# Inverting the first two chunks directly on VectorE, with loads from two queues and new due times, in a fused recurrence and MLP kernel

## The chip, the cores and the metric

One core of a Trainium2 chip runs the whole program. The metric is the device time in microseconds (us) of one execution, as the median of several. PE is TensorE, PEld its weight loads, DVE is VectorE, ACT is ScalarE, POOL is GpSimd, SP is SyncE, whose queue issues most transfers. "Clock" is TensorE's granted clock as a share of full speed. All runs quoted as fast lie within 1.5% of the fastest of the same kernel. The profiled execution is one of these runs; its span is a few us shorter than its time.

## The reference

```python
def _attn_ref(r, k, v, w, a, b):            # each [4, 8, 768, 40]
    state = zeros(B, H, D, D)
    for t in range(S):
        y[:, :, t] = einsum('bhd,bhde->bhe', rt, state)
        Sa = einsum('bhde,bhe->bhd', state, at)
        state = state * wt[..., None] - einsum('bhd,bhe->bhde', Sa, bt)
        state = state + einsum('bhd,bhe->bhde', vt, kt)
    return y

def _moe_ref(x, w_in, w_out):               # x: y as [3072, 320]
    h = x @ w_in                            # [3072, 2048]
    g = softplus(h)
    return g @ w_out
```

The kernel cuts the 768 time steps into 12 chunks of 64. Inside a chunk the recurrence becomes a triangular system, so a chunk needs the inverse of a unit triangular matrix per head and batch. Chunks hang together by the state alone. The MLP of a chunk (48 first-layer and 32 second-layer matmuls) can start when the chunk's y is there.

A word on correctness: the outputs are dominated by the MLP's weights, and y enters them weakly. The comparison therefore sees little of y.

## The kernel before

All operations are put into a graph. A list scheduler with a table of costs and a due time for each stage fixes the order on every engine when the program is built. On the chip each engine then works off its own queue in that order, waiting on semaphores:

```python
def emit(nc, stack, order):
    ...
    for o in order:
        for k, n in clock.waits(o):
            eng[o.eng].wait_ge(sem[k], n)
        ins = o.fn(o.eng)
        ...
```

Two chunks are inverted together by elimination in 60 dependent steps on GpSimd (the second engine choice, VectorE, is never taken, since chunks 0 and 1 go another way):

```python
NEUMANN = 2
NEAR = 4                       # buffers of kh, nh, gexc, aT, tlo
...
def invert(wd):
    e_, E_, cost = ("dve", V, ...) if wd == DVE_FW else ("pool", P, ...)
    op(dve(1900), [...], [mn], lambda e: V.transpose(m, mct), name="mt")
    for j in range(1, 31):
        nt = 31 - j
        op(cost(nt * j), [mn], ["mtmp"], lambda e: E_.tensor_tensor(tv, m[:, 0:j, j:j+1]..., ALU.mult))
        op(cost(nt * j), [mn, "mtmp"], [mn], lambda e: E_.tensor_tensor(m[...], m[...], tv, ALU.add))
    ...                        # mb: masked bf16 copy on the same engine
    op(dve(1100), [mbn], [dcn], ..., name="dc")     # transposed back on VectorE
    ...                        # dex: spread out, on ScalarE or VectorE
```

For chunks 0 and 1 the inverse is instead a product of powers on PE (`powers(c)`: squarings, and six apply steps in the chain). After that the chain of a chunk is W (the off-diagonal part), X, D, U, the state S and its transposes; then y, its transposes, and the MLP. All loads are issued from SyncE's queue, in a fixed list for the first four chunks; the two MLP weights come from GpSimd's queue. The MLP's h uses one PSUM bank, so ScalarE's exponential alternates with it.

Of the kernel before, what the change touches and what calls it, by code (L numbers as in the profile page):

```python
# [18 lines left out]
NEUMANN = 2  # L19
GT = 9  # L20
DVE_FW = 0
NQ = DFF // 128
# [41 lines left out]
class Graph:  # L64
# [43 lines left out]
    def deadlines(self):  # L108

        for (due, length), ops in self.stages.values():  # L110
# [7 lines left out]
PEN = 8.0  # L118
# [5 lines left out]
FILL, SAVE, MARGIN = 15000.0, 50000.0, 16  # L124
COUNT = {"tr": 8, "tot": 16, "gram": 32, "square": 32, "cum": 8, "W": 32, "X1": 16, "X": 32, "D": 32, "U": 32,
         "S1": 4, "S": 64, "sT": 32, "y1": 16, "y": 64, "yT": 6, "h": 6, "o": 4, "csb": 16, "apply": 36}
# [69 lines left out]
def schedule(ops):  # L196
# [16 lines left out]
    while ready:  # L213
# [84 lines left out]
        if o.dma:  # L298
            dmafree = max(dmafree, o.start + 900.0) + o.dma[1] * 25.4 / 16
            o.seen = dmafree + 1600.0  # L300
        else:
            o.seen = o.end + LAT[e]
# [30 lines left out]
def bass_rwkv7_goose__then__act_softplus_kernel(  # L333
# [17 lines left out]
    with ExitStack() as st:  # L351
# [51 lines left out]
        ginv = Ring("ginv", 2, [128, 2, DM], F32)  # L403
# [21 lines left out]
        mt = Ring("mt", 1, [128, 32, 32], F32)  # L425
        mtmp = sb("mtmp", [128, 240], F32)
# [17 lines left out]
        slt = sb("slt", [128, L], BF)  # L444
# [11 lines left out]
        def stage(name, i, start, length, c=None):  # L456
            g.tag = (name, i)
            g.stage = (PERIOD * ((i if c is None else c) + start), PERIOD * length)
# [10 lines left out]
        def pe(c):  # L469
            return {"pe": c}  # L470
# [21 lines left out]
        stage("const", 0, -4, 1)  # L492
# [30 lines left out]
        aff(fz[0][:, 0:128], fzn[0], 128, ALU.is_ge, 1.0, [[1, 128]], cm=-1)  # L523
        for x in X2:
            c = slice(64 * x, 64 * x + 64)
            op(dve(64), [fzn[0]], ["slt"], lambda e, c=c: V.tensor_copy(slt[c, :], fz[0][c, c]))
# [38 lines left out]

        def load(n, c):
            t, nm = RAW[n](c)
            side = F if n == "a" else G
            for bp in X2:
                for x in X2:  # L570
                    q = side(bp, x)
                    op({"sp": 800.0}, [], [nm + "%d%d" % (bp, x)],
                       lambda e, bp=bp, x=x, q=q: S.dma_start(  # L573
                           heads(t[q:q + 64, bp, :], D_),
                           SRC[n][2 * bp + x][:, c * L:(c + 1) * L, :].rearrange("h p d -> p h d")),
                       dma=(nm + "%d%d" % (bp, x), 512))

        def load_w(wd):
            t, nm = w_f(wd)
            for bp in X2:  # L580
                for x in X2:
                    q = G(bp, x)
                    op({"sp": 800.0}, [], [nm + "%d%d" % (bp, x)],
                       lambda e, bp=bp, x=x, q=q: S.dma_start(
                           heads(t[q:q + 64, bp, :], 2 * D_),
                           w[2 * bp + x][:, wd * 128:(wd + 1) * 128, :].rearrange("h (p z) d -> p h (z d)", z=2)),
                       dma=(nm + "%d%d" % (bp, x), 600))
# [5 lines left out]
        def load_weights():  # L593
            after = [kh(0)[1]]
            for q in range(3):
# [3 lines left out]
                   dma=("win%d" % q, 1500))  # L599
# [3 lines left out]
               dma=("wout", 4000))  # L603

        def setup_csb():
            stage("csb", 0, 1, 1)
# [118 lines left out]
        def logs(wd):  # L725
            stage("first", 2 * wd, -3, 1)
# [4 lines left out]
        def first(c):  # L731
            stage("first", c, -3, 1)
# [26 lines left out]
            if c < NEUMANN:  # L759
                return  # L760
# [17 lines left out]
        def power(kind, i):  # L778

            t, n = gT(i if kind == "M" else 6 + i % 2)  # L780
            return t[:, :, :].rearrange("p q m -> p (q m)").rearrange("p (b h m) -> p b h m", b=2, h=H_), n

        def powers(c):
            stage("powers", c, -0.5, 0.5)
            aT_, aTn = aT(c)
            nT_, nTn = nT(c)
            m, mn = power("M", 0)
            n, nn = power("N", 0)
            masked(grams(nT_, nTn, G, aT_, aTn, F), m, mn)
            masked(grams(aT_, aTn, F, nT_, nTn, G, F), n, nn, slt, "slt")  # L790
            for i in range(5):
                m, mn = power("M", i)
                n, nn = power("N", i)
                src, dst = (G, F) if i % 2 == 0 else (F, G)
                for kind, lhs, rhs in (("M", n, m), ("N", m, n)):
                    if kind == "N" and i == 4:
                        continue
                    t = Tile("a")

                    def f(bp, x, y, t=t, lhs=lhs, rhs=rhs, src=src, dst=dst):  # L800
                        q, o = src(bp, x), dst(bp, x)
                        return T.matmul(pf(t)[o:o + 64, bp, L * y:L * y + L], lhs[q:q + 64, bp, y, :],  # L802
                                        rhs[q:q + 64, bp, y, :])
                    op(pe(32 * 8.5), [mn, nn], [t], quads(f), mode=QUAD, name="square")
                    d, dn = power(kind, i + 1)
                    evac(1024, [t], [dn], lambda d=d: d, lambda t=t: bh(pf(t), L))


        def invert(wd):
            stage("invert", wd, -2.0, 1, 2 * wd)  # L810
            mct, mcn = mc(wd)
            m, mn = mt(wd)
            mbt, mbn = mb(wd)
# [5 lines left out]
            for j in range(1, 31):  # L819
                nt = 31 - j  # L820
                tv = mtmp[:, 0:nt * j].rearrange("p (a b) -> p a b", a=j)
                op(cost(nt * j), [mn], ["mtmp"],
# [3 lines left out]
                op(cost(nt * j), [mn, "mtmp"], [mn],  # L826
# [18 lines left out]
        def second(c):  # L845
            if c < NEUMANN:
                powers(c)
            stage("second", c, 0, 1)
# [56 lines left out]
            if c >= NEUMANN:  # L905
                t = Tile("a")

                def fw(bp, x, y, t=t):
                    q, o = F(bp, x), G(bp, x)
                    return T.matmul(pf(t)[o:o + 64, bp, L * y:L * y + 32], tl[q:q + 64, 32 * unit(bp, y):32 * unit(bp, y) + 64],  # L910
                                    de[q:q + 64, 16 * (c % 2) + unit(bp, y), 32:64])
                op(pe(32 * 8.5), [tln] + dens, [t], quads(fw), mode=QUAD, name="W")
                op(dve(512 * 1.04), [t, "wmask", "blk"], [wen],
                   lambda e, t=t: V.scalar_tensor_tensor(
                       we[:, :, :, 32:64].rearrange("p b h t -> p (b h) t"),
                       pf(t).rearrange("p b (h t) -> p (b h) t", t=64)[:, :, 0:32], blk[:, 0:1],
                       wmask[:, :].unsqueeze(1).to_broadcast([128, 16, 32]), ALU.mult, ALU.add))

            t = Tile("a")

# [32 lines left out]
            if c >= NEUMANN:  # L953
                t = Tile("a")

                def fy0(bp, x, y, t=t):
                    q, o = F(bp, x), G(bp, x)
                    return T.matmul(pf(t)[o:o + 64, bp, col(y)], de[q:q + 64, 16 * (c % 2) + unit(bp, y), :],
                                    x_[q:q + 64, bp, col(y)])
                op(pe(32 * 8.5), pair(xn) + dens, [t], quads(fy0), mode=QUAD, name="D")  # L960
                chain_evac(t, y_, yn, "De")
                t = Tile("a")

                def fu(bp, x, y, t=t):
                    q = G(bp, x)
                    return T.matmul(pf(t)[q:q + 64, bp, col(y)], we[q:q + 64, bp, y, :], y_[q:q + 64, bp, col(y)])  # L966
                op(pe(32 * 16.0), pair(yn) + [wen], [t], quads(fu), mode=QUAD, name="U")
                chain_evac(t, u_, un, "Ue")
            else:
                cur, cn, cs = x_, xn, F  # L970
                for step, (i, dst) in enumerate(((1, G), (0, F), (3, G), (2, G), (4, F), (5, G))):
                    m, mn = power("M", i)
                    nxt, nn_ = (u_, un) if step == 5 else ((y_, yn), (x_, xn))[step % 2]
                    t = Tile("a")

                    def fa(e, t=t, m=m, cur=cur, cs=cs, dst=dst):
                        for bp, x in ALL:
                            q, o = cs(bp, x), dst(bp, x)
                            T.matmul(pf(t)[o:o + 64, bp, 0:DM], eye(q), cur[q:q + 64, bp, 0:DM],
                                     start=True, stop=False)  # L980
                        for y in range(H_):
                            for bp, x in ALL:
                                q, o = cs(bp, x), dst(bp, x)
                                j = T.matmul(pf(t)[o:o + 64, bp, col(y)], m[q:q + 64, bp, y, :],
                                             cur[q:q + 64, bp, col(y)], start=False, stop=(y == H_ - 1))
                        return j
                    op(pe(290.0 + 32 * 8.5), pair(cn) + [mn, "ident"], [t], fa, mode=QUAD, name="apply")
                    chain_evac(t, nxt, nn_, "Ae")
                    cur, cn, cs = nxt, nn_, dst

# [48 lines left out]

            t = Tile("a")  # L1040
# [35 lines left out]
        def mlp(c):  # L1076
            stage("mlp", c, 1, 1)
            xT_, xTn = xT(c)
            gts = [gT(8 + c * 4 + x) for x in range(4)]
# [52 lines left out]
        for wd in range(NCH // 2):  # L1132
# [6 lines left out]
            if wd == 0:  # L1139
                pass  # L1140
            if 2 * wd >= NEUMANN:
                invert(wd)
# [44 lines left out]
```

## Time and profile before

| | before |
|---|---|
| median (3 runs given) | 393.62 us (391.86 to 393.98) |
| span of the profiled run, mean clock | 388.8 us, 0.854 |
| GpSimd's first elimination step | 93.1 us |
| first MLP matmul | 61.2 us |
| second MLP | 123.7 us |

The first part of the page gives each engine's busy time, its share of the span and its number of instructions:

```profile
PE 308.8 (79%) x8512; PEld 231.6 (60%) x8512; DVE 218.8 (56%) x360; ACT 217.0 (56%) x312; POOL 202.4 (52%) x358
```

No engine is full over the run.

### The profile page before, as it was taken

How to read it: one execution, taken by the hardware profiler on the slowest of the kernel's cores; microseconds unless marked ns; L12 is line 12 of the kernel's file. 1: busy time of each engine (PE TensorE's matmuls, PEld its weight loads, DVE VectorE, ACT ScalarE, POOL GpSimd, SP SyncE). 2: the span in 40 equal slices, each digit the busy share in tenths (PEclk: the TensorE clock that was granted, in tenths of full speed). 3: DMA queues.
4: the chain of work that ended last, by engine and by line, in shares of the span. 5: the costliest groups of instructions: out<-in, count | busy, mean ns of one | idle time of the engine just before them, and what ended most of it. 6: DMA issues, size and time to landing. Idle time of an engine off the chain costs nothing.

```text
span 388.8 us, 18635 instructions
## 1 busy us (share of the span) xinstructions
PE 308.8 (79%) x8512; PEld 231.6 (60%) x8512; DVE 218.8 (56%) x360; ACT 217.0 (56%) x312; POOL 202.4 (52%) x358
## 2 busy tenths in 40 slices
PE   0565868885688777999888869999789995999864
PEld 0454655554566445777666657777567774676542
DVE  7864642277746336676748667766663655554101
ACT  2435434557425751678865665584665747365651
POOL 6120101003989859978699954999757885000000
PEclk9855565996855988699999987999969997899997
DMA  6797996766765721476646553503202200101001
GB/s 122 123 186 139 131 150 117 141 104 111 138 104 104 120 55 27 65 120 111 120 80 110 89 96 63 88 5 71 37 19 54 55 21 3 35 4 38 18 18 34
DMA packets 145742, 31.35 MB, mean 81 GB/s; under 512 B 140224, under 2 KB 145344, under 8 KB 145664
## 3 DMA queue, kind: packets, MB, share of 16 engines
q1 hardware_dynamic: 143232, 27.55, 40.6%
q0 software_dynamic: 2432, 2.62, 4.2%
q8 instruction: 66, 1.08, 1.1%
q14 instruction: 12, 0.10, 0.1%
HBM read 28.84 MB, written 3.93 MB: 84 GB/s over the span
## 4 chain that ended last, share of the span: by engine, by line
PE 50%; DVE 15%; POOL 13%; issue 9%; ACT 8%; SPq 2%; DMA 1%; POOLq 1%; DVEq 0%; ACTq 0%
PE ps L1106 12%; PE ps L1087 11%; PE ps L636 7%; POOL mt L827 5%; POOL mtmp L823 4%; ACT gT L1096 4%; ACT et L1093 3%; POOL mb L831 2%; PE ps L698 2%; PE ps L657 2%; PE ps L802 2%; SPq L573 2%; PE ps L1056 2%; PE ps L1031 1%; PE ps L966 1%
## 5 line engine op out<-in xcount | busy, mean ns | idle before, releaser
L823 POOL TENSOR_TENSOR mtmp<-mt 128x30 f32<-128x30 f32 (+9 forms) x150 | 78.4, 523 | 57.6 <-DVE mt L818 47.1
L1093 ACT ACTIVATE et<-ps 128x512 f32<-128x512 f32 x96 | 57.1, 595 | 63.4 <-PE ps L1087 63.1
L1087 PE MATMUL ps<-xT,win 128*128 128x256 bf16 x576 | 84.6, 286 | 7.3 <-ACT et L1093 6.3
L827 POOL TENSOR_TENSOR mt<-mt,mtmp 128x30 f32<-128x30 f32 (+9 forms) x150 | 84.6, 564 | 11.0
L1106 PE MATMUL ps<-wout,gT 128*128 128x320 bf16 x384 | 68.0, 315 | 8.6 <-ACT gT L1096 7.3
L1087 PEld LDWEIGHTS ps<-xT,win 128*128 128x128 bf16 x576 | 53.5, 102 | 22.3 <-ACT et L1093 10.6
L1096 ACT ACTIVATE gT<-et,hln 128x1024 bf16<-128x1024 f32 x48 | 55.2, 1149 | 1.2
L1106 PEld LDWEIGHTS ps<-wout,gT 128*128 128x128 bf16 x384 | 34.7, 101 | 26.5 <-ACT gT L1096 10.8
L1111 DVE TENSOR_TENSOR osb<-ps,csb 128x320 f32<-128x320 f32 x24 | 11.8, 490 | 32.1 <-PE ps L1106 32.1
L889 POOL CAST v_b<-v_f 128x640 bf16<-128x640 f32 x12 | 8.6, 721 | 20.2 <-DMA v_f<-in_v_dram 18.3
L473 ACT ACTIVATE gT<-ps 128x1024 bf16<-128x1024 f32 x11 | 11.3, 1024 | 11.8 <-PE ps L802 11.7
L473 ACT ACTIVATE xb<-ps 128x320 bf16<-128x320 f32 x20 | 8.3, 435 | 17.0 <-PE ps L931 9.6
L1062 DVE TENSOR_TENSOR yo<-ps,gexc 128x640 bf16<-128x640 f32 x12 | 9.9, 825 | 12.1 <-PE ps L1056 12.0
L669 DVE TENSOR_TENSOR pt<-ps,sut 128x1024 bf16<-128x1024 f32 x12 | 14.6, 1218 | 3.7 <-PE ps L657 3.7
L669 DVE TENSOR_TENSOR qt<-ps,sut 128x1024 bf16<-128x1024 f32 x12 | 14.6, 1220 | 3.1 <-PE ps L657 3.1
L802 PE MATMUL ps<-gT 64*64 64x64 bf16 x576 | 10.2, 226 | 7.8 <-issue 4.2
L473 DVE COPY rT<-ps 128x1024 bf16<-128x1024 bf16 x10 | 6.9, 692 | 16.5 <-PE ps L636 16.5
L698 PE MATMUL ps<-lw,nexc 64*64 64x320 bf16 x96 | 8.3, 402 | 9.1 <-DVE ninc L508 9.1
L1022 DVE TENSOR_TENSOR state<-ps,gtot 128x320 bf16<-128x320 f32 x22 | 9.8, 486 | 9.1 <-PE ps L1014 9.0
L669 DVE TENSOR_TENSOR tak<-ps,sut 128x1024 bf16<-128x1024 f32 x12 | 14.6, 1215 | 0.4 <-PE ps L657 0.4
L750 DVE SCALAR_TENSOR_TENSOR nh<-b_f,ginv 128x640 bf16<-128x640 f32 x12 | 12.0, 998 | 4.7 <-ACT ginv L746 4.7
L831 POOL TENSOR_TENSOR mb<-mt,fmask 128x1024 bf16<-128x1024 f32 x5 | 13.9, 2786 | 0.4
(145 smaller groups left out, 604.3 us busy)
## 6 DMA issues: line engine op xcount, KB each, us to landing
w_f<-in_w_dram SPq DMA_DIRECT2D x24, 160.0 KB, 3.4
a_f<-in_a_dram SPq DMA_DIRECT2D x48, 80.0 KB, 3.1
b_f<-in_b_dram SPq DMA_DIRECT2D x48, 80.0 KB, 3.2
k_f<-in_k_dram SPq DMA_DIRECT2D x48, 80.0 KB, 3.1
v_f<-in_v_dram SPq DMA_DIRECT2D x48, 80.0 KB, 3.2
r_f<-in_r_dram SPq DMA_DIRECT2D x48, 80.0 KB, 3.1
out_dram<-osb SPq DMA_DIRECT2D x48, 80.0 KB, 2.1
wout<-in_moe_w_out_dram POOLq DMA_DIRECT2D x1, 1280.0 KB, 13.5
```

What stands on the lines that cost most here:

```text
L473: return A.activation(o, i, AF.Copy) if e == "act" else V.tensor_copy(o, i)
L636: i = T.transpose(pb(t)[:, bp, off + 128 * yy:off + 128 * yy + 128], src[:, bp, 128 * yy:128 * yy + 128], ident[:, :])
L669: lambda e: V.tensor_tensor(parity(dst), bh(pf(t), L), bc4(mask[:, :], L), ALU.mult), name="mask")
L698: i = T.matmul(pf(t)[s:s + 64, bp, 0:DM], mats[z][q:q + 64, :], heads(lwt[q:q + 64, bp, :], 2 * D_)[:, :, z * D_:z * D_ + D_], start=(z == ...
L802: return T.matmul(pf(t)[o:o + 64, bp, L * y:L * y + L], lhs[q:q + 64, bp, y, :], rhs[q:q + 64, bp, y, :])
L823: lambda e, j=j, nt=nt, tv=tv: E_.tensor_tensor(tv, m[:, 0:j, j:j + 1].to_broadcast([128, j, nt]), m[:, j:j + 1, j + 1:32].to_broadcast([1 ...
L827: lambda e, j=j, tv=tv: E_.tensor_tensor(m[:, 0:j, j + 1:32], m[:, 0:j, j + 1:32], tv, ALU.add))
L831: lambda e: E_.tensor_tensor(mbt[:], m[:, :, :].rearrange("p s (t e) -> p t s e", e=2), fmask[:, :, :].rearrange("p s (t e) -> p t s e", e ...
L1087: i = T.matmul(one(t)[:, 256 * (q % 2):256 * (q % 2) + 256], win[:, z, q * 128:(q + 1) * 128], xT_[:, z, :], start=(z == 0), stop=(z == 2))
L1093: lambda e, q2=q2, t=t, ett=ett: A.activation(ett[:, q2 % 2, :], one(t), AF.Exp), name="exp")
L1096: lambda e, q2=q2, ett=ett: A.activation(gts[q2 // 2][0][:, :, :].rearrange("p q m -> p (q m)"), ett[:, :, :].rearrange("p q m -> p (q m)" ...
L1106: i = T.matmul(one(t)[:, 0:DM], gts[z][0][:, q % 4, bp * 128:(bp + 1) * 128], wout[:, q, :], start=(q == 0), stop=(q == NQ - 1))
```

## The change

Its intent: the squarings of chunks 0 and 1 block the start, and GpSimd idles for 93 us. Now VectorE eliminates chunks 0 and 1 while GpSimd, as soon as it can, does 2 and 3; the squaring goes. The first loads come from two queues in the order in which the inverses need them. Every stage gets its own due time.

```diff
-NEUMANN = 2
-GT = 9
+GT = 8
 DVE_FW = 0
+FIRST = ["w0", "w2", "b0", "a0", "b1", "b2", "a1", "b3", "a2", "k0", ...]
+BY_ACT = ("a2", "b0", "b1", "v0", "v3",)
+DUE = {"const": (-5.361, 3.246), "csb": (1.398, 0.376), "logs": (-1.996, 1.066), ...}
+EARLY = {("invert", 0): -7.569, ("first", 0): -6.798, ...}
...
-        mt = Ring("mt", 1, [128, 32, 32], F32)
-        mtmp = sb("mtmp", [128, 240], F32)
+        mt = Ring("mt", 2, [128, 32, 32], F32)
+        mtmp = Ring("mtmp", 2, [128, 240], F32)
...
+        def issuers(n, c):
+            return {"act" if "%s%d" % (n, c) in BY_ACT else "sp": 680.0}
...
-        def powers(c):            # and the apply steps of the chain: all removed
...
-            if 2 * wd >= NEUMANN:
-                invert(wd)
+            invert(wd)
```

Cut: the scheduler's constants (PEN 8.0 to 10.48, the modelled sizes of transfers), the names of the stages, and a third buffer for ginv.

## The prediction

> **What bounds the kernel now.** I read, in order, the page (busy shares and the 40 slices), the longest waits, the timeline of the first 110 us, the ten-microsecond windows, and then single groups of matmuls. The slices of the page (one slice is 9.72 us; digits are busy tenths):
>
> ```profile
> PE   0565868885688777999888869999789995999864
> DVE  7864642277746336676748667766663655554101
> POOL 6120101003989859978699954999757885000000
> PEclk9855565996855988699999987999969997899997
> ```
>
> TensorE (PE) is busy 103 of the first 150 us (sum of the windows), much of that at half clock; from the 17th slice on it is nearly full. GpSimd (POOL) does nothing until slice 9, then works almost without a pause until slice 33. It runs five inversions, each for two chunks (64 steps of time each); by the timeline they lie at 93.1-133.4, 139.4-180.9, 186.9-226.9, 237.7-277.7 and 284.7-323.5 us. The waits:
>
> ```profile
> POOL mtmp L823 <- DVE mt L818: 47.1, 5, 29.7
> ...
> DVE dc L834 <- POOL mb L831: 14.7, 5, 3.9
> ```
>
> GpSimd waited 29.7 us for its first matrix, and its results were late five times. Each such lateness is a hole in PE (windows: start:end, length, PE, PEld, DVE, ACT, POOL busy, clock, DMA share, GB/s):
>
> ```profile
> 240.00:250.00 10.00, 9.60 (x346) 7.56 (x348) 6.71 (x11) 3.38 (x5) 9.01 (x17) 1.00 0.41 77
> 250.00:260.00 10.00, 9.69 (x303) 7.66 (x296) 7.17 (x12) 8.06 (x13) 8.98 (x14) 1.00 0.17 29
> ...
> 280.00:290.00 10.00, 7.05 (x152) 4.83 (x150) 6.88 (x9) 6.22 (x9) 5.11 (x14) 0.66 0.07 18
> ...
> 320.00:330.00 10.00, 5.81 (x159) 4.51 (x157) 4.83 (x7) 6.75 (x10) 5.99 (x11) 0.83 0.01 2
> ```
>
> **The start and the loads**, from the timeline (start, length):
>
> ```profile
> 0.81 2.78 SPq L584 DMA_DIRECT2D w_f<-in_w_dram  x4
> ...
> 17.17 0.82 DVE L752 TENSOR_TENSOR kh<-k_f,ginv 128x640 bf16<-128x640 f32 x1
> 18.29 1.80 POOL L598 DMA_DIRECT2D win<-in_moe_w_in_dram  x3 [11.10 <-DVE kh L752]
> ...
> 19.91 9.19 SPq L573 DMA_DIRECT2D b_f<-in_b_dram  x4
> ...
> 61.17 1.46 PE L1087 MATMUL ps<-xT,win 128*128 128x256 bf16 x6 [0.65 <-DVE xT L473]
> ```
>
> The first MLP matmul, which is the only large filler PE has, comes at 61.2 us. One queue needs about 2.7 us for four issues; chunk 1's b is fully issued only at 29.1, because the weights' transfers squeeze in. The squared-matrix route of chunks 0 and 1 then fills 20-110 us with dependent small matmuls and copies: state 1 comes at 110, the second MLP at 123.8, and chunks 2 and 3 wait for the inversion that ends at 133. By 160 us 100 of 576 first-layer matmuls are done (2.1 chunks of MLP).
>
> **PE's work at full clock.** From start-to-start times of whole groups between 160 and 340 us: six first-layer matmuls 0.655, four second-layer ones 0.545; a chunk has 8 of each, 9.6 us. The rest of a chunk: six 8-matmul transposes at 0.46 (2.8), four gram groups at 0.28 (1.1), cumulative sums and totals 1.1, W 0.55, X 0.55, D 0.28, U 0.62, state 0.93, its transposes 0.55, y 0.83, yT 0.34: also 9.6. Check: in 240-280 us there are 90 first-layer, 60 second-layer matmuls and two chunks of the rest, 1.88 x 9.6 + 2 x 9.6 = 37 of 40 us, a ratio of 1.07. In 160-340 us there are 360, 228 and eight chunks: 147 of 180 us, a ratio of 1.22. The difference is GpSimd's lateness and the clock after it.
>
> **What the Trainium skill says.** "TensorE: Matmul & The Clock Gate", Part 1: the clock is halved by default and released after some 3.4 us of activity; the trace agrees (0.50 in 20-50 us, 1.00 in 240-280). "VectorE: DVE Perf Modes", the errata section: an fp32 tensor_tensor takes (N+151)/0.96 ns; N = 640 gives 824, the trace has 815-818 with GpSimd idle. "GPSIMD Engine Reference", Specifications: its SBUF interfaces are shared with VectorE, with contention where VectorE has two SBUF inputs. The trace agrees: kh takes 0.82 us while GpSimd idles and up to 1.27 beside an inversion, and GpSimd's 240-element step, usually 0.62, took 1.08 when hit. "Trainium Kernel Development and Optimization", Key Constraints: all issuing queues share 16 DMA engines; more queues save issue time only. The trace has 122 GB/s at a DMA share of 0.66-0.77 from one queue and 177 at 0.98, so the second queue can gain at most about 1.4 times.
>
> **The change, part by part.**
> *Removed:* 576 squaring matmuls (10.2 us of PE), the apply steps (5.9 + 8.5), two gram groups (about 1); on ScalarE and VectorE their copies (11.3 and 8.6 us), four masks (4.9) and 24 half-tile copies (about 11). *Added:* W, D, U for two chunks (3.9 us of PE), and on VectorE one inversion. PE's busy time falls by about 22 us, but mostly by work in time that was half idle; what counts is the new path.
> *VectorE's inversion:* 60 tensor_tensors on 9920 elements in all: (9920 + 60 x 151)/0.96 = 19.8 us, plus 60 ns per dependent step as between its dependent memsets, 3.6: 23.4 us alone. But the order of the changed kernel puts other VectorE work inside it. The first matrix: two queues deliver a and b of chunks 0 and 1 by about 12 us; ah and nh (0.82 each), transposes at half clock (1.03), copies, grams, mc and mt (1.9) follow: the inversion starts about 25. Its first 36 steps (6384 elements, 14.5 us) are mixed with thirteen other operations (11.2 us) and in-order waits for loads, csb and wout (5 us, a guess): 56. Then mt of chunks 2 and 3 (1.9) starts GpSimd at about 58, not 93. The last 24 steps (8.8 us) and two kh (1.6) then meet GpSimd's steps: with 0.4 us each, as kh lost, another 10 us: 78. Mask, transpose and dex add 3.5, D and U to y, xT another 9: **first MLP at about 90 us, 29 us later than before.** That is the price.
> *What is gained:* at that point PE has already prepared chunks 0-3, both chains 0 and 1 are nearly through, and the next inversion is 35 us ahead. By the order of PE's instructions, left then are 12 MLPs (115), 10 chains (W, X, D, U, state and its transposes, 3.5 each: 35), 11 outputs (a transpose, a gram, y, yT, 1.9 each: 21), 10 preparations of k, v, r (three transposes, two grams, totals, 2.2 each: 22) and most of 8 of a, b (two transposes, a gram, sums, 2.05 each: 15): 208 us at full clock. GpSimd: 30-34 us of steps, 4.7 of gaps, 2.8 of mask, casts: about 41 per inversion, against about 2 x 19.2 x 1.1 = 42 of PE for two chunks. It keeps pace, tightly. I take 1.14, between 1.07 and 1.22: 237 us. The last MLP's alternation with ScalarE and the last stores add 8. Span 90 + 237 + 8 = 335. Before, the median time was 4.8 us above the profiled span (393.6 against 388.8): **340 us, 14% less.**
>
> **Rivals.** *The late first MLP decides:* if inversion, collisions and in-order waits take till 105 and the pace stays at 1.22, 105 + 254 + 13 = 372 (5% faster). For: VectorE does everything in order, and the wait for wout, which took 13.5 us to land, is inside it. Against: by 90 us the old kernel had little to show for its early start. *GpSimd stays the bound:* each of its four later inversions ends after PE wants it. From 58 us, 50 for the first with collisions and 4 x 46 give 292, then 50 us for the last two chunks (some 37 us of listed work after their D, by 1.15, and the 8 of the end): 342 span, 347 us. For: 41 against 42. Against: without the 29.7 us idle it has a head start. *Loads are hidden anyway:* the second queue brings nothing, as the shared engines are the limit; the inversion starts 5 us later: 345. *PE saturates cleanly* at 1.07 and the first MLP comes at 82: 82 + 223 + 13 = 318.
>
> **Range and chances.** First MLP 80-102 and ratio 1.07-1.22 span 316-369 at the corners; the middle 8 in 10 is 324 to 360. Being within 2% of before (over 386) needs both corners exceeded by 17 us; schedules fixed by a cost table can misfire, so 4% for same and slower together.
>
> **What would show it.** Right: GpSimd's first step at 50-65 us instead of 93; first MLP at 80-100; PE at 9 tenths or more from about 100 to the end, clock 1.00; the wait of GpSimd for mt under 25 us in total after its start; VectorE's inversion steps clearly longer after GpSimd starts. Wrong: PE holes of over 3 us before each D, at 45 us spacing (GpSimd binds); a first MLP after 105; or a long wait of VectorE for DMA within its inversion.

## The result, and the profile after

| | before | after |
|---|---|---|
| median of the same rounds (4 runs each) | 392.74 us (391.27 to 393.98) | 365.95 us (363.65 to 366.5) |
| span of the profiled run, mean clock | 388.8 us, 0.854 | 361.9 us, 0.890 |
| GpSimd's first elimination step | 93.1 us | 61.15 us |
| first MLP matmul | 61.2 us | 99.5 us |
| second MLP | 123.7 us | 121.5 us |

The ratio is 0.9318 (95% interval 0.9265 to 0.937). Ratios here are the mean time of one kernel's fast runs over that of the other's of the same rounds, so not quite the ratio of the medians quoted. The kernel is 6.8% faster; 14% was predicted, and 366 lies outside the range of 324 to 360.

The page after, busy times and the slices (one slice is 9.05 us):

```profile
PE 276.6 (76%) x7632; PEld 211.0 (58%) x7632; DVE 236.4 (65%) x415; ACT 203.1 (56%) x291; POOL 202.1 (56%) x356
...
PE   0544542048898999787999979899969999899873
...
DVE  7679729985679787676468696575954567475201
...
POOL 6010112896782078998899831899886888300000
PEclk9975855555589999999999999999996999999999
```

PE lost 32 us of busy time against the page before and the span 27. GpSimd now starts in the seventh slice. But it has two holes (slices 13 and 14, 24 and 25), which an engine that binds would not have, and PE's clock is at half from the sixth to the eleventh slice although PE is busy at eight tenths in the last two of these. From there up to the last slices PE has 6 to 9 tenths, not a steady 9.

The start, in the timeline (start, length, then what ended the idle time before it):

```profile
27.44 0.19 DVE L812 TENSOR_TENSOR mtmp<-mt 128x30 f32<-128x30 f32 x1
...
52.10 0.82 DVE L773 TENSOR_TENSOR kh<-k_f,ginv 128x640 bf16<-128x640 f32 x1 [7.10 <-DMA k_f<-in_k_dram]
...
61.15 0.29 POOL L812 TENSOR_TENSOR mtmp<-mt 128x30 f32<-128x30 f32 x1 [10.97 <-DVE mt L807]
...
73.83 2.34 PE L719 MATMUL ps<-lw,ninc 64*64 64x320 bf16 x16 [17.13 <-ACT lw L750]
...
74.17 0.66 DVE L812 TENSOR_TENSOR mtmp<-mt 128x30 f32<-128x30 f32 x1
...
79.02 0.62 PE L946 MATMUL ps<-xb,dex 64*64 64x40 bf16 x32 [2.85 <-DVE dex L831]
...
99.48 1.46 PE L1054 MATMUL ps<-xT,win 128*128 128x256 bf16 x6
```

VectorE's inversion starts at 27.4 and its result enters D at 79.0. In between it stands 7.1 us for k, and its last steps run beside GpSimd's: a step on 30 elements took 0.19 us at the start and 0.66 us at 74.2. PE waits 17 us for a logarithm of chunk 4, whose w landed late. From D to the first MLP it takes 20.5 us.

The windows (start:end, length, PE, PEld, DVE, ACT, POOL busy, clock, DMA share, GB/s):

```profile
80.00:90.00 10.00, 8.10 (x310) 7.11 (x308) 5.32 (x11) 3.37 (x6) 6.59 (x12) 0.50 0.90 165
90.00:100.00 10.00, 8.50 (x261) 6.51 (x254) 6.70 (x8) 4.48 (x8) 7.86 (x11) 0.50 0.56 104
...
240.00:250.00 10.00, 9.90 (x268) 7.47 (x267) 5.42 (x10) 6.30 (x10) 9.06 (x15) 1.00 0.33 62
250.00:260.00 10.00, 10.00 (x328) 8.17 (x329) 8.36 (x12) 7.26 (x12) 9.14 (x14) 1.00 0.26 45
260.00:270.00 10.00, 7.10 (x108) 4.66 (x96) 6.74 (x8) 5.21 (x8) 8.63 (x19) 1.00 0.15 34
280.00:290.00 10.00, 9.52 (x385) 7.22 (x383) 6.33 (x11) 4.27 (x8) 8.93 (x15) 1.00 0.53 94
```

In 80-100 us PE looks busy, at half clock. In 260-270 there is a hole like those of the kernel before: the D of chunk 8 (270.5) waits for GpSimd's fourth inversion, which ended at 265.1.

The waits (engine, operation, line, then what it waited for; us in total, times, longest):

```profile
ACT et L1060 <- PE ps L1054: 49.2, 53, 3.0
...
PE ps L719 <- ACT lw L750: 29.5, 2, 17.1
POOL v_b L876 <- PE ps L980: 26.5, 5, 10.5
...
POOL mtmp L812 <- DVE mt L807: 19.6, 3, 11.0
...
DVE dc L823 <- POOL mb L820: 5.0, 3, 3.0
```

GpSimd waited 19.6 us for its matrices, 47.1 before, of which 11.0 are the start. It also waited 26.5 us before casts of v, which stand in its queue behind PE's state product. By the timeline GpSimd's inversions lie at 61.1-106.8, 127.6-166.9, 170.0-208.4, 225.8-265.1 and 268.1-307.5. So the gaps are 20.8, 3.1, 17.4 and 3.0 us; each holds the masked copy mb, which takes 2.8 us on GpSimd.

**Where PE's time went.** I multiplied every matmul of the trace with the unit cost of the prediction (W at its full-clock 0.27 us, see below). From 100 to 340 us that gives 191 of 240 us. The other 49 us are: 19.3 at 178 places where PE goes from full-array to quarter-array tiles or back without any idle time (0.11 us each), 25.4 at 34 places where it idles, and 4.4 spread thin.

### The profile page after: what moved, and what is told of

The parts are those of the page before. It is cut to its first block, busy times and chain, and to the rows that moved or that the text cites. A ratio compares the mean times of both kernels' runs of the same rounds, so it can differ in the third digit from the quotient of the medians.

```text
span 361.9 us, 16900 instructions
## 1 busy us (share of the span) xinstructions
PE 276.6 (76%) x7632; PEld 211.0 (58%) x7632; DVE 236.4 (65%) x415; ACT 203.1 (56%) x291; POOL 202.1 (56%) x356
## 4 chain that ended last, share of the span: by engine, by line
PE 34%; POOL 23%; DVE 16%; ACT 8%; issue 7%; SPq 5%; ACTq 3%; DMA 2%; POOLq 1%; DVEq 0%
POOL mt L816 10%; POOL mtmp L812 10%; PE ps L1054 9%; PE ps L1073 9%; PE ps L657 5%; SPq L594 4%; ACT gT L1063 3%; DVE mtmp L812 3%; ACTq L594 2%; DVE mt L816 2%; DVE mt L807 2%; PE ps L954 2%; PE ps L678 2%; PE ps L980 2%; ACT et L1060 2%
## 5 line engine op out<-in xcount | busy, mean ns | idle before, releaser
L812 POOL TENSOR_TENSOR mtmp<-mt 128x30 f32<-128x30 f32 (+9 forms) x150 | 79.2, 528 | 30.2 <-DVE mt L807 19.6
L816 POOL TENSOR_TENSOR mt<-mt,mtmp 128x30 f32<-128x30 f32 (+9 forms) x150 | 83.0, 553 | 11.1
L1054 PE MATMUL ps<-xT,win 128*128 128x256 bf16 x576 | 81.1, 278 | 5.5 <-ACT et L1060 4.5
L1073 PE MATMUL ps<-wout,gT 128*128 128x320 bf16 x384 | 63.7, 300 | 6.7 <-ACT gT L1063 4.2
L1054 PEld LDWEIGHTS ps<-xT,win 128*128 128x128 bf16 x576 | 51.9, 99 | 17.6 <-ACT et L1060 8.4
L876 POOL CAST v_b<-v_f 128x640 bf16<-128x640 f32 x12 | 8.6, 717 | 37.2 <-PE ps L980 26.5
L719 PE MATMUL ps<-lw,ninc 64*64 64x320 bf16 x96 | 11.3, 371 | 17.1 <-ACT lw L750 17.1
L750 ACT ACTIVATE lw<-w_f 128x1280 bf16<-128x1280 f32 x6 | 7.6, 1273 | 22.5 <-DMA w_f<-in_w_dram 13.5
L719 PEld LDWEIGHTS ps<-lw,ninc 64*64 64x64 bf16 x96 | 5.8, 132 | 19.8 <-ACT lw L750 17.3
L773 DVE TENSOR_TENSOR kh<-k_f,ginv 128x640 bf16<-128x640 f32 x12 | 12.1, 1008 | 7.1 <-DMA k_f<-in_k_dram 7.1
L771 DVE SCALAR_TENSOR_TENSOR nh<-b_f,ginv 128x640 bf16<-128x640 f32 x12 | 14.3, 1190 | 2.2 <-ACT ginv L767 2.2
L876 POOL CAST r_b<-r_f 128x640 bf16<-128x640 f32 x12 | 9.3, 775 | 10.6 <-DMA r_f<-in_r_dram 9.8
```

Source lines behind the costliest of these rows:

```text
L719: i = T.matmul(pf(t)[s:s + 64, bp, 0:DM], mats[z][q:q + 64, :], heads(lwt[q:q + 64, bp, :], 2 * D_)[:, :, z * D_:z * D_ + D_], start=(z == ...
L771: lambda e: V.scalar_tensor_tensor(hd(n_), bh(bf_, D_), -1.0, bh(gi, D_), ALU.mult, ALU.mult))
L812: lambda e, j=j, nt=nt, tv=tv: E_.tensor_tensor(tv, m[:, 0:j, j:j + 1].to_broadcast([128, j, nt]), m[:, j:j + 1, j + 1:32].to_broadcast([1 ...
L816: lambda e, j=j, tv=tv: E_.tensor_tensor(m[:, 0:j, j + 1:32], m[:, 0:j, j + 1:32], tv, ALU.add))
L876: lambda e, dst=dst, src=src: P.tensor_copy(hd(dst), bh(src, D_)), name="cast")
L1054: i = T.matmul(one(t)[:, 256 * (q % 2):256 * (q % 2) + 256], win[:, z, q * 128:(q + 1) * 128], xT_[:, z, :], start=(z == 0), stop=(z == 2))
```

## The experiments

Each kernel ran beside the kernel before, whose median was 389 to 395 us, most on different chips; so ratios are compared with the changed kernel's 0.9318, and differences under about 1% are not resolved. Unless the text says that the order is another, it is frozen on every engine as in the changed kernel: the scheduler keeps its old costs, and only what the chip does changes. All runs behind the ratios are fast ones; the medians are of all four runs, with one slow run in warm_through, two in local_four and one in local_five.

| run | median us | ratio to before | 95% interval |
|---|---|---|---|
| changed kernel | 365.95 | 0.9318 | 0.9265 to 0.937 |
| old_no_squaring | 380.8 | 0.975 | 0.9683 to 0.9818 |
| one_queue | 373.71 | 0.958 | 0.95 to 0.9661 |
| pool_light | 357.28 | 0.9169 | 0.9097 to 0.924 |
| mlp_light | 367.88 | 0.9431 | 0.9366 to 0.9496 |
| mlp_thin | 364.27 | 0.9287 | 0.9244 to 0.9331 |
| both_light | 351.08 | 0.8926 | 0.8853 to 0.8998 |
| mlp_heavy | 374.18 | 0.957 | 0.9504 to 0.9636 |
| dve_light | 363.94 | 0.9231 | 0.9161 to 0.9302 |
| fast_start | 370.7 | 0.9405 | 0.9321 to 0.9489 |
| warm | 367.49 | 0.9357 | 0.9317 to 0.9397 |
| warm_through | 374.32 | 0.9549 | 0.9459 to 0.9639 |
| cast_act | 363.73 | 0.9312 | 0.9246 to 0.9379 |
| cast_dve | 365.88 | 0.9369 | 0.9301 to 0.9436 |
| due_search | 373.97 | 0.9535 | 0.9507 to 0.9564 |
| local_four | 383.04 | 0.9712 | 0.963 to 0.9795 |
| local_five | 380.5 | 0.9716 | 0.9669 to 0.9764 |

### Which part of the change brings what

**old_no_squaring**: the kernel before with the inversion on VectorE alone (the scheduler ran anew on it, with the old due times).

```diff
-NEUMANN = 2
-GT = 9
+NEUMANN = 0
+GT = 8
-        mt = Ring("mt", 1, ...); mtmp = sb("mtmp", ...)
+        mt = Ring("mt", 2, ...); mtmp = Ring("mtmp", 2, ...)
```

> The kernel before with one part of the change alone: chunks 0 and 1 inverted on VectorE like the others on GpSimd, no squaring, the rings of the inversion's tiles as in the changed kernel; loads and due times stay as they were. If the inversion on VectorE is the part that brings the gain: 360 to 375 us. If the due times and load order carry it: 385 to 400 us, with GpSimd's first step still near 90 us.

**one_queue**: the changed kernel with all loads issued from SyncE.

```diff
         order = schedule(g.ops)
+        for o in order:
+            if o.dma and o.eng == "act":
+                o.eng = "sp"
```

> The changed kernel with every load issued from SyncE's queue, in the same order; nothing else changes. My prediction's rival (loads hidden anyway, the 16 shared engines are the limit): 366 to 371 us, the first MLP matmul at 99 to 104 us. If the second queue matters: the inversion on VectorE starts 5 or more later than 27.4 us and the time is 372 or more. If the loads on ScalarE's own queue cost more than they bring (ScalarE's first Ln waited till 11.1 us behind its twelve issues, 6.4 in the kernel before): under 364 us.

Measured: 380.8 and 373.7. GpSimd's first step in the timeline of old_no_squaring, then of one_queue:

```profile
74.97 0.83 POOL L824 TENSOR_TENSOR mtmp<-mt 128x30 f32<-128x30 f32 x1 [11.37 <-DVE mtmp L824]
```

```profile
67.82 0.28 POOL L812 TENSOR_TENSOR mtmp<-mt 128x30 f32<-128x30 f32 x1 [10.64 <-DVE mt L807]
```

So the step goes from 93.1 to 75.0 by leaving the squaring out, to 67.8 by the new order and due times (with a third buffer for ginv), and to 61.15 by the second queue; the ratio goes 1, 0.975, 0.958, 0.9318. All three parts count, with 2.5, 1.7 and 2.6 points (the first is clear of 1 by its interval, but not surely over 2%). My expectation for old_no_squaring missed both its ranges; that for one_queue got the time right, but VectorE's inversion started at 30.9, 3.5 us later and not 5. The rival "loads are hidden anyway" (5 us in the prediction) falls: the second queue is worth 2.6 points, some 10 us. The order of one_queue was made for two queues, though; an order of its own might lose less, and was not run. The price of the second queue is visible too. ScalarE issues twelve loads before its first logarithm, which starts at 11.09 us, 6.38 in the kernel before (timelines, before and after):

```profile
6.38 1.27 ACT L729 ACTIVATE lw<-w_f 128x1280 bf16<-128x1280 f32 x1 [4.30 <-DMA w_f<-in_w_dram]
...
11.09 1.27 ACT L750 ACTIVATE lw<-w_f 128x1280 bf16<-128x1280 f32 x1 [9.00 <-issue]
```

### What sets the pace: GpSimd, PE or neither

**pool_light** (wrong result): GpSimd's steps on one row.

```diff
-                       tv, m[:, 0:j, j:j + 1]...
+                u = 1 if wd != DVE_FW else j
+                       tv[:, 0:u, :], m[:, 0:u, j:j + 1]...     # the addition likewise
```

> The changed kernel, but each elimination step on GpSimd works on one row instead of j rows (same instructions, order and waits; the result is wrong on purpose). GpSimd's inversions then take about 20 instead of 39.5 us. Theory GpSimd (its inversions, with the ring of four buffers behind them, set the pace of PE): 15 us or more faster than the changed kernel, 350 us or less. Theory PE (PE's own work, mode switches and in-order queue set the pace, GpSimd only fits in): within 6 us, 360 to 366 us. It also takes away GpSimd's collisions with VectorE, worth some us in either theory.

**mlp_light** (wrong): two contraction parts instead of three.

```diff
-                        for z in range(3):
+                        for z in range(2):
```

> The changed kernel with two instead of three contraction parts in each first-layer matmul group: 192 of 576 such matmuls less, 0.11 us each, 21 us of PE work removed, same order (the result is wrong on purpose). Theory PE: 16 to 21 us faster than the changed kernel, 345 to 350 us. Theory GpSimd: PE's gaps before each D only grow, 0 to 8 us faster, 358 to 366 us.

**mlp_thin** (wrong): the third part on 32 columns, with every instruction kept.

```diff
+                            n = 256 if z < 2 else 32
-                            i = T.matmul(one(t)[:, 256 * (q % 2):256 * (q % 2) + 256], ..., xT_[:, z, :], ...)
+                            i = T.matmul(one(t)[:, 256 * (q % 2):256 * (q % 2) + n], ..., xT_[:, z, 0:n], ...)
```

> As the light MLP, but with the number of instructions kept: the third contraction part of each first-layer group works on 32 of 256 columns, 17 us of PE's streaming less (wrong result on purpose). The light MLP brought nothing, but it also shifted where PE's instruction stream is fetched. If PE's work does not set the pace: 362 to 368 again. If the shift of the stream hid a gain: 350 to 358.

**both_light**: pool_light and mlp_thin together.

> The changed kernel with GpSimd's elimination steps on one row and, on PE, the third contraction part of each first-layer matmul cut to 32 of 256 columns (same instruction count, order and waits on every engine; 17 us of PE's streaming removed; wrong result on purpose). So far half of GpSimd's work removed brought 1.5%, a tenth of PE's brought nothing. Theory two bounds (GpSimd and PE each close behind the other): both together bring more than the sum, 340 us or less on the changed kernel's 366. Theory fixed order (a loop over all engines, chunk c+4 waiting through buffers and in-order queues for chunk c, in which neither amount counts): no more than the light GpSimd alone, 355 to 361 us.

**mlp_heavy** (wrong): a fourth matmul in each first-layer group.

```diff
-                        for z in range(3):
+                        for n, z in enumerate((0, 0, 1, 2)):
```

> The changed kernel with a fourth matmul in every first-layer group (the first contraction part twice, so the result is wrong on purpose): 192 matmuls more, 21 us of PE's streaming added, the order unchanged. Taking 17 to 21 us away brought 1 us or nothing. If PE lies close behind the loop through GpSimd (5 to 8 us of slack over the run, by the light GpSimd): 12 to 16 us slower, 378 to 382. If PE has much room: under 5 us slower, below 371.

Measured, against 0.9318: light GpSimd 1.6% faster, thin PE 0.3% (not resolved; the light variant, which also has fewer instructions, came out 1.2% slower, for a reason that stays open), both together 4.2%, heavy PE 2.7% slower. In us by the ratios, times 393: about 6, 1, 15, and 10 of the 21 that were added. PE's work can shrink without effect, and half of what is added comes through; GpSimd's work can be halved for 6 us. Neither theory is right as I put it. With both light the gain exceeds the sum (15 against 7), which speaks for two close bounds; but 351 is not the 340 that this theory asked for.

In pool_light GpSimd, with light steps, did not run ahead, as its longest wait shows:

```profile
POOL v_b L877 <- PE ps L981: 68.3, 10, 10.8
```

The casts of v stand inside its inversions and wait for PE's state product, 68 us over the run. So in pool_light its steps run from 124.7 to 156.7 in the second inversion, and from the start of that to the start of the fourth it is 97.4 us, 98.2 in the changed kernel; from the third to the fifth it is 94.8 against 98.1. So the period of four chunks shrinks by 1 to 3 us, although the steps of an inversion fell from some 32 to some 15 us in sum. Half of the 6 us won is the start: VectorE's own inversion, beside GpSimd's lighter steps, ended at 70.4 instead of 75.1, and D of chunk 2 came at 112.6 instead of 115.6. The same two periods are 98.8 and 98.9 us in mlp_thin, 103.2 and 102.1 in mlp_heavy, and 93.3 and 91.8 in both_light: it shrinks by far the most when both are light.

**cast_act** and **cast_dve**: the casts of chunks 2 to 11 on another engine. Both results are right.

```diff
+        for o in order:
+            if o.name == "cast" and o.tag[1] >= 2:
+                o.eng = "act"          # or "dve"
```

> The changed kernel with the casts of v and r of chunks 2 to 11 done by ScalarE instead of GpSimd, each at the same place of the modelled time; the result stays right. GpSimd loses about 15 us of work and the waits for PE's state product inside its queue (26.5 us over the run). If GpSimd's queue sets the pace: each inversion 3 us shorter or earlier, 355 to 361. If the casts only move the wait to ScalarE, which then holds the MLP's exponentials: 366 or more.

> As the previous one, with VectorE doing the casts. If GpSimd's queue sets the pace: 355 to 361. If VectorE, which makes GpSimd's next matrix and the masks, is the tighter one: 366 to 372.

Measured: 0.9312 and 0.9369, no gain. The waits of cast_act:

```profile
POOL mtmp L812 <- DVE mt L807: 51.6, 3, 25.3
```

GpSimd's first inversion now ended at 100.3 instead of 106.8, and its second began at 128.7, 1.1 us later than in the changed kernel. The 6 us won went into the wait for mt. In the changed kernel that wait was partly booked on the cast that stood in front. What held the result is in VectorE's queue in cast_act's timeline:

```profile
100.56 2.78 POOL L820 TENSOR_TENSOR mb<-mt,fmask 128x1024 bf16<-128x1024 f32 x1
...
109.55 0.81 DVE L1030 TENSOR_TENSOR yo<-ps,gexc 128x640 bf16<-128x640 f32 x1
110.28 0.81 DVE L771 SCALAR_TENSOR_TENSOR nh<-b_f,ginv 128x640 bf16<-128x640 f32 x1
111.01 0.82 DVE L773 TENSOR_TENSOR kh<-k_f,ginv 128x640 bf16<-128x640 f32 x1
111.74 1.04 DVE L823 STREAM_TRANSPOSE dc<-mb 128x512 f32<-128x512 f32 x1
```

GpSimd's mb was done at 103.3, but dc, the next step, began at 111.7, as in the changed kernel (111.8). It stands behind other work in VectorE's queue, at its end yo of chunk 1 and nh and kh of chunk 5; VectorE was busy in 6.90 of the 8.4 us between. That nh and kh stand behind yo has to do with their four buffers; that dc stands behind them is the order alone. In this order an earlier inverse cannot be used. D of chunk 2 comes at 115.6 in the changed kernel and at 116.7 here: ScalarE's dex came 1.1 us later (113.96 instead of 112.83), with a moved cast of r just before it. Later D of chunk 8 came 3.3 us earlier (267.2), but only 1.7 of these were left at the end, which the runs do not resolve. In this place at least, the order of the queues is why a lightened engine brought nothing.

### The first MLP

**dve_light** (wrong): pool_light's edit for VectorE's inversion.

> The changed kernel, but VectorE's own inversion works on one row instead of j rows (same instructions, order and waits; wrong result on purpose), which takes about 8 us out of its 27 to 75 us alone. If the start counts in full: GpSimd's first step at 55 to 58 and the time 5 to 8 us less, 358 to 361. If VectorE waits for loads there anyway: GpSimd's first step within 2 us of 61 and 364 to 367.

**fast_start**: weights and column sums later, w of chunks 4 and 5 earlier.

```diff
+        move(lambda o: o.dma and o.dma[0].startswith("win"), step1)
+        move(lambda o: o.dma and o.dma[0] == "wout", step1)
+        move(lambda o: o.tag[0] == "csb", lambda o: o.name == "h")
+        move(lambda o: o.tag == ("load w", 4), lambda o: o.tag == ("load a", 4))
```

> The changed kernel with the order of three groups of loads changed: both MLP weights are issued just before GpSimd's first elimination step instead of at 18 and 37 us, the column sums that need the second weight move to just before the first MLP on PE and VectorE, and w of chunks 4 and 5 is loaded before a of chunk 4. Theory: VectorE's inversion stands 7 us waiting for k behind the weights' transfers, and PE 5 us for wout; then GpSimd's first step comes 5 to 10 us earlier than 61 us and the first MLP at 88 to 94 instead of 99.5; the time falls by as much, 356 to 361 us. Rival (the start does not count, or the clock and VectorE decide it): within 2 us of the changed kernel, 364 to 368.

Measured: dve_light brought D of chunk 0 from 79.0 to 74.9 and the first MLP to 97.1, and 0.9% (not resolved). GpSimd's first step moved by only 1.2 us. In fast_start it did come at 53.8, inside what I expected, and nothing was won (0.9405). The first MLP came at 105.0. The issues of the weights have no wait of their own, so they left GpSimd's queue at 37.8 to 39.6, not at its first step. So only wout moved. GpSimd's waits for r in fast_start, and the second of the two in its timeline:

```profile
POOL r_b L876 <- DMA r_f<-in_r_dram: 25.2, 2, 15.6
...
68.75 0.72 POOL L876 CAST r_b<-r_f 128x640 bf16<-128x640 f32 x1 [9.53 <-DMA r_f<-in_r_dram]
```

The longer one lay before the inversion (till 34.2 us). The other lay inside it: a cast of r stood 9.5 us for its load, where the cast of r at 67.0 in the changed kernel did not wait. So the inversion, begun 7.4 us earlier, ended at 109.3, 2.5 us later than in the changed kernel. That the weights crowded this load out is likely, but was not shown.

**warm**: idle matmuls where PE waits for the logarithm.

```diff
+        def warm_(e):
+            for z in range(104):
+                i = T.matmul(psf[:, bank, 0:DM], ones[:, :], wout[:, z % 16, :], start=True, stop=True)
+        order.insert(i, o)             # before PE's first operation of chunk 4
```

> The changed kernel with 104 matmuls on data of no use (320 columns each, into an idle bank) put on PE before its first wait for chunk 4's logarithm, where PE stands still from 57 to 74 us. Theory: the granted clock of 0.50 between 50 and 100 us is what made the way from D of chunk 0 (79.0) to the first MLP (99.5) 20.5 us long instead of the 12 I predicted; with the clock up it takes 13 to 16, the first MLP comes at 92 to 96, and the time falls by 3 to 7 us (359 to 363). Rival (waits for VectorE, ScalarE and the in-order queue, not the clock): the way stays 19 to 21 us and the time within 2 us of 366.

**warm_through**: also 24 before D, and 4 before every second operation up to the first MLP.

```diff
+        for j in [l4, d0] + list(range(d0 + 2, h0, 2)):
+            o = warm_(104 if j == l4 else 24 if j == d0 else 4)
+            order.insert(order.index(pes[j]), o)
```

> As the warmed kernel, but the idle matmuls go on: 104 before the wait for chunk 4's logarithm, 24 before D of chunk 0, and 4 before every second PE operation from D to the first MLP. In the warmed kernel the clock rose to 1.00 at 60-70 us and fell back to 0.50 at 80-100, and nothing was gained. Theory clock: with 0.9 or more granted over 80-100 us the way from D to the first MLP takes 15 us or less although about 5 us of idle matmuls lie in it, and the time is 361 to 365. Rival (in-order waits): the way takes 21 or more, the time 366 to 371.

(The expectation of warm says "the 12 I predicted"; the record has 3.5 for mask to dex and 9 from D to the MLP, so 9 is the number to compare with.) Measured: 0.9357 and 0.9549. The window 80-90 us in warm, then in warm_through:

```profile
80.00:90.00 10.00, 8.47 (x326) 7.23 (x322) 4.95 (x9) 3.76 (x5) 5.88 (x10) 0.50 0.79 147
```

```profile
80.00:90.00 10.00, 8.78 (x370) 6.31 (x369) 5.08 (x11) 2.65 (x5) 7.44 (x12) 1.00 0.82 149
```

In warm the clock was 1.00 at 60-70 us. It fell back at 76.9, in the 3.6 us in which PE stood still before D, and in 80-100 us, with PE busy 8.47 and 8.97 of 10, it stayed at 0.50: the small matmuls of the chains did not bring it back. Whether they would have held it is not shown. In warm_through it stayed at 1.00 from 70 to 110 us. In warm D to the MLP took 20.8 us. In warm_through it took 20.4, but 44 idle matmuls of 0.134 us (5.9 us) lay in it, so 14.5 without them (the changes of tiles that they add not taken off). As a whole the way was neither 15 or less nor 21 or more; as an estimate, the half clock made some 6 of the 20.5 us. A kernel that pays for the clock with idle matmuls in the path gains nothing.

### What a change of tiles costs

**switch_test**: a measurement appended after the last matmul; a single run, of unknown state.

```diff
+        few = [full_(8), quad_(8)] * 8
+        for fn in [wide_(48), full_(64), quad_(64)] + few + [full_(64), quad_(64)] + few:
+            ...                        # appended to PE's queue
```

> The changed kernel with a measurement appended on PE after its last matmul: 48 wide matmuls to warm up, then twice (64 full-array matmuls, 64 quarter-array ones; then the same 128 in turns of 8). From the trace of the changed kernel I read 0.11 us lost per change between full and quarter tiles (178 changes, 19.3 us). If that is a cost of the change itself, the sixteen turns take 14 x 0.11 = 1.5 us longer than the two blocks; if it was only waiting that happened to lie there, under 0.4 us longer.

The timeline of switch_test, full-array then quarter-array groups:

```profile
365.15 2.03 PE L1130 MATMUL ps<-ones,ident 128*128 128x64 bf16 x64
367.11 0.71 PE L1138 MATMUL ps<-ones,ident 64*64 64x64 bf16 x64
367.75 0.41 PE L1130 MATMUL ps<-ones,ident 128*128 128x64 bf16 x8
368.09 0.26 PE L1138 MATMUL ps<-ones,ident 64*64 64x64 bf16 x8
```

From start to start the two blocks took 2.602 us and the same 128 matmuls in sixteen turns 4.216: 1.614 us more for 14 more changes, 0.115 each, with the clock at 1.00 and nothing to wait for. So a change costs this much by itself. The 19.3 us in the changed kernel, 0.108 at each place, agree with it, though the tiles there have other sizes as well.

### Can another order do better

**due_search**: other due times and load order, found by a search over a replay of the queues (the scheduler ran anew, so the order is another).

```diff
-PEN = 10.48
+PEN = 6.80
-BY_ACT = ("a2", "b0", "b1", "v0", "v3",)
+BY_ACT = ('a2', 'b0', 'b1', 'r2', 'v0', 'v2')
 ...                                   # all of FIRST, DUE and EARLY
```

> The changed kernel's program with other due times and another order of the first loads, found by a search over them against durations read from the traces (a replay of the queues, with one full pass of collisions and late transfers); no operation is added or removed. It holds GpSimd's first inversion back until VectorE's own is nearly done. Theory (the order on the in-order queues is what the 49 lost us come from): 8 to 15 us faster than the changed kernel, 351 to 358. Rival (the replay misses what binds: clock, instruction fetch): within 4 us, 362 to 370.

**local_four** and **local_five**: single operations moved, without and with a fifth buffer.

```diff
+SHIFT = {...}                         # us earlier or later, operation by operation
-        gexc = Ring("gexc", NEAR, ...)
+        gexc = Ring("gexc", 5, ...)   # local_five only; kh and nh likewise, gT 6
```

> The changed kernel with nothing added or removed: only single operations moved a few microseconds earlier or later in their engines' queues, by a hill climb on a replay of the queues with durations read from the traces (the replay gives 361 for it and 372 for the changed kernel; it failed once, for the searched due times). Theory (the fixed order loses the time, near the tuned order a small move is well predicted): 5 to 11 us faster than the changed kernel, 355 to 361. Rival (tuned on the chip already; the replay lacks what binds): within 3 us, 363 to 369, or slower.

> As the previous one, with a fifth buffer for kh, nh and the exponential of chunk sums, so that chunk 5's are free after y of chunk 0 and not of chunk 1 (room from six instead of eight of the MLP's g buffers), and its own hill climb (358 by the replay). If the ring of four buffers holds the loop: 3 us or more faster than local_four and GpSimd's second inversion starts before 122 us instead of 127.6. If the ring is not what binds: within 3 us of local_four.

Measured: 0.9535, 0.9712 and 0.9716, all slower, where my replay had promised 8 to 15 us. due_search is instructive: its first MLP comes at 88.2, 11 us earlier, and D of chunk 0 at 69.7; but GpSimd starts at 70.7, the second MLP comes at 120.5, and from the first MLP to the end it takes 284 us instead of 262. An earlier first MLP is thus worth nothing in itself. Some runs of the two local kernels, the profiled ones among them, were slow (over 1.5% above their fastest), so I don't read their traces. Their times are equal, which shows no gain from a fifth buffer; but each has an order of its own, so it does not clear the ring of four buffers either. No version beat the changed kernel with a right result by more than the noise.

## Why the prediction was wrong

The direction was right, the size was not: span 361.9 instead of 335. The sum has two parts, and both failed: the first MLP came at 99.5 instead of 90 (9.5), and the rest took 262.4 instead of 245 (17.4). Each lay inside the span that the prediction gave for it (80 to 102, and in the sum's own terms 252 over 208, a ratio of 1.21); both lay on the late side, and so the whole fell outside 324 to 360, though not outside the 369 of the corners.

- *VectorE's inversion starts about 25, GpSimd about 58, VectorE's ends at 78*: right; 27.4, 61.15 and 75.1. The collisions were there, but smaller: the last 24 steps and two kh took 14 us, not 20. VectorE's 30-element step took 0.19 us alone and 0.66 beside GpSimd. A long wait of VectorE for a load within its inversion, named as a sign against, did occur: 7.1 us for k.
- *"D and U to y, xT another 9"*: failed, 20.5. I counted the dependent path to the first MLP, not PE's queue. In the changed order PE has 23 operations from D of chunk 0 up to the first MLP, 12 of them of chunk 1. By the unit costs they are 9.1 us at full clock, and so 18 at half clock, which is what the windows grant until 100 us. I had read the 0.50 in the kernel before and did not apply it; I had even noted that the trace agrees with a clock that activity releases, although PE was busy 9.21 of 10 us in 40-50 us there, at 0.50. That the work of the 23 operations also comes to 9 is a coincidence: the predicted 9 was meant for another, shorter path. In warm_through, at 1.00, the same way took 14.5 us without the idle matmuls: at full clock the waits come out that the slow PE had covered, and the clock alone is worth some 6 us.
- *"I take 1.14, between 1.07 and 1.22"*: failed, and it is the larger term. The 208 us of work took 252 us, from 99.5 to 352; by the finer count above the ratio is 1.26 from 100 to 340 us (240 over 191). Both ends of the range were miscounted in the kernel before: I had counted the chunks "of the rest" by their state products, two in 240-280 us and eight in 160-340. Matmul by matmul the first window holds 34.3 of 40 us, so 1.17, and the second about 136 of 180, so 1.32 (with some 23 us at half clock in it). The kernel before was thus slower over its work than I thought, and the changed one, with 1.26, is no slower than that. Midway between the two right readings, 1.245, the same sum gives 259 us for this part, 7 above what was measured. (W's 0.55 in the list was a reading at half clock; at full clock it takes 0.27.) Of the 49 us lost from 100 to 340 us, 19.3 are changes between tile modes, a term that I had not seen. It is not new, though: in 160-340 us the kernel before has 146 such places, 0.81 per us, the changed one 0.74 in 100-340; so a ratio read rightly would have contained it. 25.4 are idle places.
- *"It keeps pace, tightly"* for GpSimd: half right. The inversion took 38.4 to 39.4 us, or 45.7 for the first, against the 41 predicted. But 20.8 and 17.4 us passed before its second and fourth, 2.8 of each for mb, and D of chunks 2, 4, 6, 8 and 10 each came 5 to 9 us after the inversion before it ended. The rival "GpSimd stays the bound" (347) had the holes right and the reason at least not whole: in cast_act GpSimd ended its first inversion 6.5 us earlier, and D of chunk 2 came no earlier.
- *"The last MLP's alternation and the last stores add 8"*: 10, from the 12 us of streaming in the last 21.9 us.
- *Removed and added work*: right in direction, low in size: PE's busy time fell by 32 us, and I had said about 22. A busy sum counts half-clock time too, and the mean clock rose from 0.854 to 0.890; the difference was not followed up.
- *Loads hidden anyway*, a rival at 345: fell; one_queue is 2.6 points slower.
- *The late first MLP decides*, a rival at 372: the nearest in number, and right that the in-order waits count; yet due_search shows that the first MLP's time by itself does not decide.

What the form of the sum (first MLP, plus work, times a ratio) hides is what makes the ratio. The order is fixed at build, every queue is in order, and a loop goes through all engines: y of chunk c, then nh and kh of c+4 on VectorE, transposes and grams on PE, mt on VectorE, the inversion on GpSimd, dc on VectorE, D on PE. The dc of one pair stands behind the nh of a later one. Shown are these: with light GpSimd steps the period of four chunks is 97.4 and 94.8 us instead of 98; PE's work can shrink without effect; with both light the period is 93.3 and 91.8; in cast_act dc waits 8 us in VectorE's queue. Whether two close bounds or this loop describes that better was not settled. Only argued is how much of the 25 us of idle places an order or a buffer could win back: three attempts lost 8 to 16 us, so the order of the changed kernel is better than my replay could find, and whether the ring of four buffers or the order itself holds the loop stays open.

## What to carry to other kernels

In a program whose order is fixed at build, count what stands in each queue between two events, at the clock granted there, and not only the dependent path between them; and count the changes of PE's tile mode as work. A pace read from a window of the old kernel is only as good as the count of the work in it: count every matmul, not one product per chunk. Lightening one engine at a time with the order frozen is a cheap test for a bound: if neither alone helps and both do, look for what stands in front of the result in the next engine's queue. A wait is booked on whatever stands at the head of an in-order queue; move that away and see where the wait goes before calling it the cause.

## What the Trainium skill lacked or had wrong

- "TensorEngine Tiling (Array Packing)", Key Properties, says that a change of the tiling mode drains TensorE, but has no time for it. Here it is 0.115 us between full-array and quarter-array matmuls of 64 columns (14 changes, 1.614 us), and 178 places with such a change lose 19.3 us in 240.
- "TensorE: Matmul & The Clock Gate", Part 1, says that some 3.4 us of sustained activity release the clock. Here PE was busy 8.10 and 8.50 of 10 us in two windows one after the other, in small matmuls, and was granted 0.50 in both; with 24 wide matmuls before D and 4 before every second operation after it, 1.00 was granted. Part 1 does not say how much counts as activity; Part 4 says only that transpose-mode matmuls do not count in the same way.
- "GPSIMD Engine Reference", Specifications, names the contention with VectorE but not its size (other pages describe how one excludes the other, without figures for steps as small as these): VectorE's 30-element elimination step went from 0.19 to 0.66 us, while the steps of GpSimd's first inversion took 34.3 us in sum beside VectorE's, 30.1 to 33.1 in the four later ones.
- None of the pages that I read says what loads on ScalarE's queue cost ScalarE's own work: its first logarithm waited 9.00 us behind the issues and started at 11.09 instead of 6.38 us, while the second queue still brought 2.6 points.
